# Top-32 attention and a gated MoE on one core: where the weight-decoding steps and the slot masks stand in the turns of the start-up

## The chip, the core and the metric

The kernel runs on one core of a Trainium2 chip, as a single program with one launch. The metric is the device time of that program in microseconds (us). The engines are TensorE (PE, with its weight loads as PEld), VectorE (DVE), ScalarE (ACT), GpSimd (POOL) and SyncE (SP, which here only issues DMAs). Each engine executes its own instructions strictly in the order in which the program lists them; between engines only semaphores order the work.

## The reference

Eight batches of eight heads, 576 positions, head size 64. Every query keeps its 32 best scores, and the attended values go through a product of two projections and two more projections:

```python
scores = q @ k.T / 8                      # per batch and head: 576 x 576
kth    = 32nd largest of each row
attn   = softmax(where(scores >= kth, scores, -1e9))
x      = (attn @ v)                       # gathered to 4608 x 512
h      = (x @ w1) * (x @ w2)              # 4608 x 1024
out    = (h @ w3) @ w_out                 # 4608 x 512
```

All inputs and the result are 32-bit floats.

## The kernel before

**Attention slots.** The work of the attention is cut into 144 slots of 128 queries for two streams of scores (a pair of heads, or the two ends of a pair of pairs). The main loop (line 529) makes one turn for each `p` from -1 to 146, and a turn works on four slots at once, at four different stages. In this document turn n is the pass with p = n. For slot p (`top32_steps`, lines 245 to 272), DVE reduces the scores to three sorted sets and takes eight maxima four times. For slot p - 1, POOL makes the two bounds of a row, `edge` (line 274), ACT and POOL make the mask (`mask`, line 301: a Relu on ACT, then a subtraction on POOL, once for each half), ACT takes the exponentials with their sums (`exps`, line 306), POOL adds 1e-9 to the sums (`enlarge`), DVE inverts them (`invert`), and POOL multiplies (`normalise`, line 316). For slot p - 2, PE turns the weights (`turn`, tiles `tp` and `ro`), ACT copies them, PE forms the values, and ACT and DVE split these into a high and a low part, `xf`. For slot p + 1, PE forms the scores (`st`) and ACT copies them to `s`.

**Filling.** The MoE of a finished part of a batch (`moe_steps`, line 368, tiles `ab` and `eo`) is a generator of matmuls. `fill` (line 493) is called three times in a turn and lets as many matmuls of it onto PE as the table `SHARE` allows. The MoE can begin only when the weights are decoded.

**Weight units.** The weights arrive as 64-bit floats in 40 tiles `z` of 512 KB, fetched by SP three ahead (`prefetch`, line 509), into four buffers. Each tile is a *unit*: a generator that does one step whenever it is advanced. Its steps (`decode`, line 113, and the loaders at lines 142, 156 and 166) are, in order: for some units (`by_pool`) a scaling on POOL, `y<-z`, from which only the sign is used; two conversions on ACT, `t<-z` and `z<-z`; one or two bit operations on DVE, `y<-t` and `y<-t,y`; an addition on POOL, `y<-y,z` (or `wo<-y,z`); and for w1 and w2 a rounding on ACT, `wh<-y`, and a subtraction on POOL, `wl<-y,wh`. The w3 units are then multiplied with w_out on PE, in eight products `pf` for each of eight results, which ACT and DVE split into `wf`.

**Where the steps stand.** `warm` (line 514) starts at most one new unit and advances every unit under way by one step. It is called at five places of each turn (lines 547, 559, 566, 583 and 594), and in turn -1 at two of them (lines 583 and 594). Nothing else sets the order: what a call of `warm` emits goes to each engine ahead of all that the loop emits after it. The five places are: in the first stage, ahead of the masks of slot p - 1; behind `turn`; behind the second `fill`; behind `enlarge`, ahead of `normalise`; and at the end of the turn, behind `normalise`, so ahead of the `edge` of the next turn.

The start-up ends when the last unit has done its last step, between the `normalise` of turn 14 and the bounds of turn 15; from there on `warm` does nothing.

Of the kernel before, what the change touches and what calls it, by code (L numbers as in the profile page):

```python
# [60 lines left out]
def attn_moe(ctx: ExitStack, tc: tile.TileContext, q, k, v, w1, w2, w3, w_out, out, flag, general):  # L61
# [45 lines left out]
    def fetch(src):  # L107

        z = z_p.tile([128, 1024], F32, tag="z", name="z")
        sp.dma_start(z.bitcast(I32), src)  # L110
        return z
# [49 lines left out]
    def weigh(n):  # L161
        while heavy and n:
            heavy.pop(0)()
            n -= 1
# [31 lines left out]
    def load_qk(b, part, hp):  # L196

        lo, n, _ = PARTS[part]
        qt = kq_p.tile([128, NA], F32, tag="q", name="qt")
        sp.dma_start(qt[:, :n], at(q, b, hp)[:, lo : lo + n])  # L200
        kt = kq_p.tile([128, S + 64], F32, tag="k", name="kt")
        sp.dma_start(kt, at(k, b, hp))
        return qt, kt

    def load_v(b, hp):

        vt = kq_p.tile([128, 11 * D], F32, tag="v", name="vt")
        sp.dma_start(vt, at(v, b, hp))
        return vt
# [22 lines left out]
    def new_s():  # L232
        return att_p.tile([128, 2, S], F32, tag="s", name="s", bufs=2)

    def take_scores(s, st, h):
        lo, hi = KEYS[h]
        return act.copy(s[:, :, lo:hi], st[h][:, :, : hi - lo])
# [7 lines left out]
    def top32_steps(s, st, taken, slot):  # L245

        w = att_p.tile([128, 2, S], F32, tag="w", name="w", bufs=1)
        top = tops[slot % len(tops)]
        one, two, three = slice(0, NG), slice(NG, 2 * NG), slice(2 * NG, S)
        in_two, in_three = st[0][:, :, NG : 2 * NG], st[1][:, :, :NG]
        dve.tensor_tensor(w[:, :, three], s[:, :, one], in_two, op=ALU.max)
        dve.tensor_tensor(w[:, :, two], s[:, :, one], in_two, op=ALU.min)
        yield
        ins = dve.tensor_tensor(w[:, :, one], w[:, :, three], in_three, op=ALU.max)
        behind(ins, taken, "one engine at a time reads a bank of the scores")  # L260
        dve.tensor_tensor(w[:, :, three], w[:, :, three], in_three, op=ALU.min)
        yield
        for i in range(4):
            cut = slice(i * 8, (i + 1) * 8)
            for a in range(2):
                dve.max(top[:, a, cut], w[:, a, one] if i < 3 else w[:, a, :])
                if i == 3 and a == 0:
                    yield
            if i < 3:
                for a in range(2):  # L270
                    dve.match_replace(w[:, a, one], top[:, a, cut], w[:, a, one], NEG)
                yield

    def edges_of(slot):
        top = tops[slot % len(tops)]
        edge = small.tile([128, 2, 2], F32, tag="edge", name="edge")
        pool.tensor_tensor(edge, top[:, :, 0:32:31], coef, op=ALU.mult)
        return edge

    def compare(slot):  # L280
        top = tops[slot % len(tops)]
        pool.tensor_tensor(over[:, 2 * slot : 2 * slot + 2], top[:, :, 31], top[:, :, 23], op=ALU.subtract)
# [15 lines left out]
    def new_weights():  # L298
        return att_p.tile([128, 2, S], F32, tag="pab", name="pab"), small.tile([128, 2], F32, tag="sums", name="sums")

    def mask(s, edge, pab, a):

        act.activation(pab[:, a, :], s[:, a, :], AF.Relu, bias=edge[:, a, 1:2], scale=-STEEP)
        pool.tensor_tensor(pab[:, a, :], s[:, a, :], pab[:, a, :], op=ALU.subtract)

    def exps(edge, pab, sums, a):
        p = pab[:, a, :]
        act.activation(p, p, AF.Exp, bias=edge[:, a, 0:1], scale=SCALE, accum_out=sums[:, a : a + 1])
# [11 lines left out]
    def turn(pab):  # L320

        tp = ps_a.tile([128, 2, 512], F32, tag="a", name="tp")
        flat = pab[:].rearrange("p a c -> p (a c)")
        for a in range(2):
            for c in range(4):
                o = a * (S + 64) + c * 128
                pe.transpose(tp[:, a, c * 128 : (c + 1) * 128], flat[:, o : o + 128], ident)
        ro = ps_v.tile([128, 512], F32, tag="v", name="ro")
        pe.transpose(ro[:, :128], flat[:, 512:640], ident)
        return tp, ro  # L330

    def take_turned(tp, ro):
        pts = att_p.tile([128, 2, 512], F32, tag="pts", name="pts", bufs=1)
        act.copy(pts, tp)
        pr = att_p.tile([128, 128], F32, tag="pr", name="pr")
        act.copy(pr, ro[:, :128])
        return pts, pr
# [26 lines left out]
    def take_low(to, ov):  # L364
        for x, cols, n in to:
            dve.tensor_tensor(x[:, 1, cols], ov[:, n], x[:, 0, cols].bitcast(F32), op=ALU.subtract)
# [122 lines left out]
    def evict():  # L489
        while put_off:  # L490
            put_off.pop(0)()

    def fill(n):
        nonlocal spare
        evict()
        spare = spare + n if queue else 0
        while queue and spare > 0:
            cost = next(queue[0], None)
            if cost is None:
                queue.pop(0)  # L500
            elif not cost:
                spare = 0
            else:
                spare -= cost

    waiting = list(startup)
    fetched, going, turns = [], [], []

    def prefetch(n):
        while waiting and len(fetched) < n:  # L510
            src, step = waiting.pop(0)
            fetched.append((fetch(src), step))

    def warm(first=True):

        if p < 0 and not first:
            return
        turns.append(p)
        n = len(turns)
        if fetched and (n % 5 if n < 11 else n % 2) and len(going) < 5:  # L520
            z, step = fetched.pop(0)
            going.append(step(z))
        going[:] = [unit for unit in going if next(unit, "end") != "end"]
        prefetch(3)

    qk[units[0]] = load_qk(*units[0])
# [2 lines left out]
    for p in range(-1, n_slots + 3):  # L529
        i, j, m = p + 1, p - 1, p - 2  # L530
        if i < n_slots:
            for u in units:
                if first[u] - 2 == i:
                    qk[u] = load_qk(*u)
                if first[u] == i:
                    vts[u] = load_v(u[0], u[2])
        finder = top32_steps(ss[p], *sts.pop(p), p) if 0 <= p < n_slots else iter(())
        if 0 <= j < n_slots:
            edges[j] = edges_of(j)
        next(finder, None)  # L540
        if m - 1 in lows:
            take_low(*lows.pop(m - 1))
            b, part, _ = slots[m - 1][0][0]
            if final[b, part] == m - 1:
                queue.append(moe_steps(b, part, [xts.pop((b, part, hp)) for hp in range(NHP)], put_off.append))
        next(finder, None)
        if p >= 0:
            warm()
        if 0 <= j < n_slots:
            pabs[j] = new_weights()  # L550
            for a in range(2):
                mask(ss[j], edges[j], pabs[j][0], a)
            compare(j)
        fill(SHARE[0])
        next(finder, None)
        if 0 <= m < n_slots:
            tp, ro = turn(pabs[m][0])
            pts, pr = take_turned(tp, ro)
        warm(False)
        if 0 <= j < n_slots:  # L560
            exps(edges[j], *pabs[j], 0)
            exps(edges[j], *pabs[j], 1)
        weigh(1)
        fill(SHARE[1])
        next(finder, None)
        warm(False)
        if i < n_slots:
            st = scores([qk[u] for u in slots[i][0]], slots[i][1])
            ss[i] = new_s()
            take_scores(ss[i], st, 0)  # L570
            sts[i] = st, take_scores(ss[i], st, 1)
        if 0 <= m < n_slots:
            us, t = slots[m]
            for u in us:
                if u not in xts:
                    xts[u] = new_x()
            ov = values([vts[u] for u in us], t, pts, pr, ro)
            lows[m] = places([xts[u] for u in us], t), ov
            take_high(*lows[m])
        if 0 <= j < n_slots:  # L580
            enlarge(pabs[j][1])
        next(finder, None)
        warm()
        next(finder, None)
        if 0 <= j < n_slots:
            invert(pabs[j][1])
            normalise(*pabs[j])
        weigh(8)
        fill(SHARE[2])
        for _ in finder:  # L590
            pass
        if 0 <= m < n_slots:
            del ss[m], pabs[m], edges[m]
        warm()
# [62 lines left out]
```

## Time and profile before

| | |
|---|---|
| time, median of 3 runs | 1267.78 us (1266.63 to 1267.80) |
| the profiled execution's own time | 1266.87 us |
| its span, first to last instruction | 1264.9 us |
| PE busy | 1209.7 us (96%) |
| DVE busy | 1135.0 us (90%) |
| ACT busy | 943.4 us (75%) |
| POOL busy | 872.4 us (69%) |

The span is what the trace covers; the execution's own time is 2.0 us longer. Busy shares are means over the whole span, and the start-up of some 200 us looks different from the rest: the page's slices show PE at 3 to 8 tenths in the first six slices (of 31.6 us each), and at 9 in nearly all the later ones. An idle time in a listing stands in brackets behind the instruction that it precedes, with the operation that ended it.

### The profile page before, as it was taken

The numbers are of one execution on the slowest core, as the hardware profiler recorded it, in microseconds if no ns is written. First come the engines' busy times: TensorE is split into PE (matmuls) and PEld (weight loads), VectorE is DVE, ScalarE is ACT, GpSimd is POOL, SyncE is SP. The second block draws the span as 40 slices with busy tenths as digits, with TensorE's granted clock in tenths as the row PEclk, the third lists the DMA queues.
The fourth block names the chain that finished last, engine by engine and source line by source line (L and its number), as shares of the span: only waits on it lengthen the run. The fifth ranks groups of instructions, "written<-read, shape, count | busy, mean of one in ns | idle before, by whom it ended". The sixth has DMA issues, their size and how long they took to land.

```text
span 1264.9 us, 29916 instructions
## 1 busy us (share of the span) xinstructions
PE 1209.7 (96%) x10513; PEld 1043.5 (82%) x10513; DVE 1135.0 (90%) x3968; ACT 943.4 (75%) x2025; POOL 872.4 (69%) x1213
## 2 busy tenths in 40 slices
PE   3788889999999999999999999999999999999998
PEld 1444568888888888888888888888888888888898
DVE  7897979999999999999999999999999999999910
ACT  5887877777777777777777777777777777777731
POOL 5887887676766767676766767676766767676731
PEclk9999989999999999999999999999999999999999
DMA  7533421202112121202112121202112111202000
GB/s 236 174 129 130 156 70 40 91 27 70 55 39 90 36 63 40 90 28 70 55 39 91 36 63 40 90 28 70 55 39 91 35 63 40 91 27 70 13 22 21
DMA packets 42803, 85.92 MB, mean 68 GB/s; under 512 B 4754, under 2 KB 21138, under 8 KB 42642
## 3 DMA queue, kind: packets, MB, share of 16 engines
q1 hardware_dynamic: 42642, 83.91, 20.6%
q8 instruction: 85, 1.39, 0.5%
q14 instruction: 76, 0.62, 0.2%
HBM read 74.45 MB, written 9.44 MB: 66 GB/s over the span
## 4 chain that ended last, share of the span: by engine, by line
PE 75%; POOL 10%; DVE 7%; ACT 4%; issue 3%; DMA 1%; SPq 0%; DVEq 0%; POOLq 0%; ACTq 0%
PE ab L52 27%; PE eo L52 15%; PE ro L52 12%; PE st L52 11%; PE tp L52 9%; POOL pab L52 5%; DVE w L52 3%; DVE top L52 2%; ACT pab L52 2%; PE pf L52 2%; POOL y L52 2%; POOL g L52 1%; DVE y L52 1%; POOL wl L52 1%; ACT pts L52 1%
## 5 line engine op out<-in xcount | busy, mean ns | idle before, releaser
L52 POOL TENSOR_TENSOR pab<-s,pab 128x576 f32<-128x576 f32 x288 | 404.8, 1427 | 121.9 <-ACT pab L52 121.9
L52 DVE MAX8 top<-w 128x8 f32<-128x192 f32 (+1 forms) x1152 | 478.5, 448 | 0.0
L52 PE MATMUL ab<-xf,wh 128*128 128x256 f32 (+1 forms) x2048 | 438.5, 302 | 10.1 <-DVE y L52 8.7
L52 PEld LDWEIGHTS ab<-xf,wh 128*128 128x128 f32 x2048 | 332.9, 189 | 21.6 <-DVE y L52 9.5
L52 ACT ACTIVATE pab<-s,edge 128x576 f32<-128x576 f32 x288 | 208.0, 769 | 176.6 <-POOL edge L52 176.6
L52 PE MATMUL ab<-xf,wl 128*128 128x256 f32 (+1 forms) x1024 | 307.4, 300 | 0.0
L52 DVE MATCH_REPLACE8 w<-top,w 128x192 f32<-128x192 f32 x864 | 289.7, 343 | 0.0
L52 POOL TENSOR_SCALAR pab<-pab,sums 128x576 f32<-128x576 f32 x288 | 212.6, 751 | 78.0 <-DVE sums L52 78.0
L52 ACT ACTIVATE pab<-pab,edge 128x576 f32<-128x576 f32 x288 | 223.1, 779 | 11.9 <-POOL pab L52 9.7
L52 PE MATMUL eo<-g,wf 128*128 128x256 f32 (+1 forms) x1536 | 231.6, 301 | 0.0
L52 PEld LDWEIGHTS eo<-g,wf 128*128 128x128 f32 x1536 | 208.5, 188 | 8.1 <-issue 7.5
L52 PEld LDWEIGHTS ab<-xf,wl 128*128 128x128 f32 x1024 | 193.4, 189 | 4.1 <-issue 4.1
L52 PE MATMUL st<-kt,qt 64*128 64x192 f32 (+3 forms) x1280 | 182.8, 435 | 9.8 <-DMA kt<-in_k 4.8
L52 ACT COPY pts<-tp 128x1024 f32<-128x1024 f32 x144 | 145.6, 1011 | 46.8 <-PE tp L52 44.3
L52 ACT COPY s<-st 128x768 f32<-128x768 f32 (+1 forms) x288 | 169.9, 646 | 5.8 <-PE st L52 5.8
L52 PE MATMUL tp<-ident,pab 128*128 128x128 f32 x1152 | 153.8, 278 | 14.2 <-DVE w L52 9.5
L52 PEld LDWEIGHTS st<-kt,qt 64*128 64x128 f32 (+1 forms) x1280 | 97.9, 178 | 83.7 <-issue 18.6
L52 DVE TENSOR_TENSOR w<-w,st 128x384 f32<-128x384 f32 x288 | 158.2, 549 | 4.9
L52 PE MATMUL ro<-pts,vt 128*64 128x128 f32 (+1 forms) x2560 | 161.2, 269 | 1.0 <-ACT pr L52 1.0
L52 DVE TENSOR_TENSOR w<-s,st 128x384 f32<-128x384 f32 x288 | 146.7, 551 | 14.0
L52 POOL TENSOR_TENSOR g<-whole,g 128x256 fp32r<-128x256 f32 (+1 forms) x128 | 103.3, 807 | 78.6 <-ACT g L52 78.6
L52 PEld LDWEIGHTS ro<-pts,vt 128*64 128x64 f32 x2560 | 127.5, 137 | 34.4 <-issue 24.2
(47 smaller groups left out, 1128.7 us busy)
## 6 DMA issues: line engine op xcount, KB each, us to landing
vt<-in_v SPq DMA_DIRECT2D x64, 352.0 KB, 3.2
kt<-in_k SPq DMA_DIRECT2D x64, 320.0 KB, 3.8
z<-in_w SPq DMA_DIRECT2D x32, 512.0 KB, 3.8
qt<-in_q SPq DMA_DIRECT2D x32, 160.0 KB, 3.2
out_t<-osb SPq DMA_DIRECT2D x32, 160.0 KB, 1.8
z<-in_wo SPq DMA_DIRECT2D x8, 512.0 KB, 5.2
qt<-in_q SPq DMA_DIRECT2D x32, 128.0 KB, 3.1
out_t<-osb SPq DMA_DIRECT2D x32, 128.0 KB, 1.7
```

The source lines that it names most:

```text
L52: ins = fn(*args, **kw)
```

## The change

Three things are changed, all in the order of emission; no instruction is added or taken away.

- In `warm`, a newly started unit does its first step ahead of the steps of the older units, where before it came last.
- In the first stage of a turn, the masks of slot p - 1 and the small `compare` on POOL come ahead of the call of `warm`, where before they came behind it.
- In turn -1 only the call at the end of the turn remains, so that one unit has been started ahead of slot 0 where before there were two. All later starts thereby move by one call of `warm`.

```diff
@@ warm
         turns.append(p)
-        n = len(turns)
+        n, new = len(turns), None
         if fetched and (n % 5 if n < 11 else n % 2) and len(going) < 5:
             z, step = fetched.pop(0)
-            going.append(step(z))
+            new = step(z)
+            next(new)
         going[:] = [unit for unit in going if next(unit, "end") != "end"]
+        if new:
+            going.append(new)
         prefetch(3)
@@ first stage of a turn
         next(finder, None)
-        if p >= 0:
-            warm()
         if 0 <= j < n_slots:
             pabs[j] = new_weights()
             for a in range(2):
                 mask(ss[j], edges[j], pabs[j][0], a)
             compare(j)
+        if p >= 0:
+            warm()
         fill(SHARE[0])
@@ last stage of a turn
             enlarge(pabs[j][1])
         next(finder, None)
-        warm()
+        if p >= 0:
+            warm()
         next(finder, None)
```

How this moves instructions is shown on POOL at three places. There `edge` are the bounds of a slot, `pab<-s,pab` its two masks, `sums<-sums` its `enlarge`, and `pab<-pab,sums` its `normalise`; rows with `z`, `wl` or `wo` are steps of units.

POOL in turn 3, from the bounds to the `enlarge`, before:

```order
L52 TENSOR_TENSOR edge_395<-top2_100,coef_93 128x4
L52 TENSOR_TENSOR pab_406<-s_270,pab_406 128x576 x2
L52 TENSOR_TENSOR over_96<-top2_100 128x2
L52 TENSOR_TENSOR wl00_106<-y_348,wh0_101 128x512
L52 TENSOR_TENSOR y_389<-y_389,z_282 128x512
L52 TENSOR_SCALAR y_434<-z_309 128x512
L52 TENSOR_SCALAR sums_407<-sums_407 128x2
```

and now:

```order
L52 TENSOR_TENSOR edge_388<-top2_100,coef_93 128x4
L52 TENSOR_TENSOR pab_396<-s_266,pab_396 128x576 x2
L52 TENSOR_TENSOR over_96<-top2_100 128x2
L52 TENSOR_TENSOR y_373<-y_373,z_254 128x512
L52 TENSOR_SCALAR y_439<-z_335 128x512
L52 TENSOR_TENSOR wl00_106<-y_373,wh0_101 128x512
L52 TENSOR_TENSOR y_403<-y_403,z_290 128x512
L52 TENSOR_SCALAR sums_397<-sums_397 128x2
```

The scaling of the new unit (`y_434<-z_309`, now `y_439<-z_335`) has moved ahead of the two steps of older units, and a further addition (`y_373`) that stood ahead of the bounds now stands behind the masks.

POOL from a `normalise` to the masks of the next turn, before, at the change from turn 6 to turn 7:

```order
L52 TENSOR_SCALAR pab_740<-pab_740,sums_741 128x576 x2
L52 TENSOR_TENSOR wl00_106<-y_734,wh0_101 128x512
L52 TENSOR_TENSOR y_777<-y_777,z_666 128x512
L52 TENSOR_SCALAR y_830<-z_707 128x512
L52 TENSOR_TENSOR edge_838<-top0_98,coef_93 128x4
```

and now, at the change from turn 5 to turn 6:

```order
L52 TENSOR_SCALAR pab_620<-pab_620,sums_621 128x576 x2
L52 TENSOR_SCALAR y_711<-z_596 128x512
L52 TENSOR_TENSOR wl00_106<-y_627,wh0_101 128x512
L52 TENSOR_TENSOR y_664<-y_664,z_543 128x512
L52 TENSOR_TENSOR edge_720<-top2_100,coef_93 128x4
```

The same three steps stand between the `normalise` and the bounds, one turn earlier, and the scaling is now the first of them. At the change from turn 6 to turn 7 none is left between the two.

POOL from the `normalise` of turn 13 to the `enlarge` of turn 14, before:

```order
L52 TENSOR_SCALAR pab_1535<-pab_1535,sums_1536 128x576 x2
L52 TENSOR_TENSOR g_1404<-whole_1641,g_1404 128x320
L52 TENSOR_TENSOR edge_1658<-top1_99,coef_93 128x4
L52 TENSOR_TENSOR wl11_1602<-y_1578,wh1_102 128x512
L52 TENSOR_TENSOR y_1633<-y_1633,z_1461 128x512
L52 TENSOR_TENSOR pab_1672<-s_1469,pab_1672 128x576 x2
L52 TENSOR_TENSOR over_96<-top1_99 128x2
L52 TENSOR_TENSOR wl11_1602<-y_1633,wh1_102 128x512
L52 TENSOR_TENSOR y_1668<-y_1668,z_1516 128x512
L52 TENSOR_SCALAR sums_1673<-sums_1673 128x2
```

and now:

```order
L52 TENSOR_SCALAR pab_1524<-pab_1524,sums_1525 128x576 x2
L52 TENSOR_TENSOR g_1396<-whole_1635,g_1396 128x320
L52 TENSOR_TENSOR wl11_1627<-y_1531,wh1_102 128x512
L52 TENSOR_TENSOR y_1596<-y_1596,z_1433 128x512
L52 TENSOR_TENSOR edge_1655<-top1_99,coef_93 128x4
L52 TENSOR_TENSOR pab_1663<-s_1461,pab_1663 128x576 x2
L52 TENSOR_TENSOR over_96<-top1_99 128x2
L52 TENSOR_TENSOR wl11_1627<-y_1596,wh1_102 128x512
L52 TENSOR_TENSOR y_1649<-y_1649,z_1487 128x512
L52 TENSOR_SCALAR sums_1664<-sums_1664 128x2
```

The two steps that stood between the bounds and the masks stand ahead of the bounds now; the number of steps from the `normalise` to the `enlarge` is the same.

Counted over the `normalise` of turns 1 to 14, 22 unit steps of POOL stood between one of them and the next masks; now it is 13.

On PE the order changes only in the `pf` products of the start-up: they come in groups of other sizes, the last eight all in turn 11, where four of the last eight stood in turn 10. The first `ab` matmul stands between the `tp` of turns 11 and 12 in both, and from there on PE's order is the same. From turn 16 on no engine's order differs.

## Rows read from the trace of the kernel before

**Rows 1.** Stretches: from:to, length, busy (instructions) of PE, PEld, DVE, ACT, POOL; clock, DMA.
```profile
47.00:124.00 77.00, 66.83 (x371) 34.82 (x368) 66.06 (x197) 59.12 (x118) 61.85 (x74) 0.96 0.43 142
124.00:171.00 47.00, 38.98 (x235) 27.34 (x233) 43.19 (x129) 39.26 (x78) 41.68 (x47) 0.93 0.44 140
...
201.00:1264.90 1063.90, 1056.31 (x9598) 946.90 (x9596) 962.51 (x3447) 792.99 (x1730) 712.97 (x1020) 1.00 0.17 53
```

**Rows 2.** Waits of DVE from 8 to 201 us: total us, times, longest.
```profile
DVE y L52 <- ACT t L52: 13.9, 5, 8.2
DVE sums L52 <- POOL sums L52: 4.0, 5, 2.2
DVE y L52 <- POOL y L52: 3.2, 2, 2.5
DVE y L52 <- ACT xf L52: 2.5, 1, 2.5
DVE wf L52 <- ACT wf L52: 1.3, 2, 0.8
DVE whole L52 <- ACT asb L52: 1.0, 1, 1.0
```

**Rows 3.** Timeline of DVE, rows with idle time before them: start, us, instruction, [idle <-releaser].
```profile
49.93 0.69 DVE L52 SCALAR_TENSOR_TENSOR y<-t,y 128x512 int32<-128x512 int32 x1 [2.47 <-POOL y L52]
...
88.02 0.69 DVE L52 TENSOR_TENSOR wf<-pf,wf 128x512 fp32r<-128x512 f32 x1 [0.77 <-ACT wf L52]
...
92.17 0.69 DVE L52 TENSOR_SCALAR y<-t 128x512 int32<-128x512 int32 x1 [0.51 <-ACT t L52]
...
108.08 0.69 DVE L52 TENSOR_SCALAR y<-t 128x512 int32<-128x512 int32 x1 [2.30 <-ACT t L52]
...
120.57 0.69 DVE L52 SCALAR_TENSOR_TENSOR y<-t,y 128x512 int32<-128x512 int32 x1 [2.46 <-ACT xf L52]
...
164.57 0.69 DVE L52 TENSOR_SCALAR y<-t 128x512 int32<-128x512 int32 x1 [1.90 <-ACT t L52]
...
169.90 0.69 DVE L52 TENSOR_SCALAR y<-t 128x512 int32<-128x512 int32 x1 [0.95 <-ACT t L52]
...
181.24 0.17 DVE L52 RECIPROCAL sums<-sums 128x2 f32<-128x2 f32 x1 [2.23 <-POOL sums L52]
...
191.42 0.17 DVE L52 RECIPROCAL sums<-sums 128x2 f32<-128x2 f32 x1 [0.88 <-POOL sums L52]
```

**Rows 4.** Timelines of ACT and DVE at the start: the first copy of scores, the first comparison.
```profile
6.50 1.18 ACT L52 COPY s<-st 128x768 f32<-128x768 f32 x2 [4.49 <-PE st L52]
...
9.57 1.01 DVE L52 TENSOR_TENSOR w<-s,st 128x384 f32<-128x384 f32 x2
```

**Rows 5.** Timeline of POOL in turn 3.
```profile
46.71 1.28 POOL L52 TENSOR_TENSOR wl<-y,wh 128x512 fp32r<-128x512 f32 x1
47.94 1.30 POOL L52 TENSOR_TENSOR y<-y,z 128x512 int32<-128x512 int32 x1
49.21 0.69 POOL L52 TENSOR_SCALAR y<-z 128x512 f32<-128x512 f32 x1
```

**Rows 6.** Timeline of POOL: the bounds and the masks of turn 7.
```profile
88.85 0.21 POOL L52 TENSOR_TENSOR edge<-top,coef 128x4 f32<-128x4 f32 x1
89.94 2.79 POOL L52 TENSOR_TENSOR pab<-s,pab 128x576 f32<-128x576 f32 x2 [0.89 <-ACT pab L52]
```

**Rows 7.** Waits of POOL from 8 to 201 us.
```profile
POOL pab L52 <- ACT pab L52: 8.1, 10, 1.3
```

**Rows 8.** Timeline of PE: seven products (two records each); the first `ab`.
```profile
129.42 6.28 PE L52 MATMUL pf<-wo,y 128*128 128x512 f32 x14
...
145.71 0.56 PE L52 MATMUL ab<-xf,wh 128*128 128x320 f32 x2 [2.99 <-DVE y L52]
```

**Rows 9.** Timeline of PE: the eight turning matmuls of turns 3 and 4.
```profile
41.50 1.94 PE L52 MATMUL tp<-ident,pab 128*128 128x128 f32 x8 [5.56 <-DVE w L52]
...
54.40 1.06 PE L52 MATMUL tp<-ident,pab 128*128 128x128 f32 x8
```

## Prediction

> **What bounds the kernel now.** I read the busy times by stretch first [rows 1]. From 201 us on PE is busy 1056.31 of 1063.90 us, and its order there is not touched: this part costs what it did. From 47 to 171 us PE, DVE, ACT and POOL are all busy 77% to 92% of their time: PE 66.83 of 77.00 us in the first stretch, DVE 66.06, then DVE 43.19 of 47.00. No engine is full, so waits between them set the time. So the change can only move the moment at which the start-up hands over to the PE-bound part.
>
> The waits of DVE come second [rows 2]. Without the 8.2 us before its first instruction, DVE waits 5.7 + 4.0 + 3.2 + 2.5 + 1.3 + 1.0 = 17.7 us up to 201 us: for the conversions of units (`t`), for the sums, for POOL's scalings, and for `wf`. None of these is a wait at the first instruction of a turn, for scores: DVE paces the turns, and what delays it is what the turns last too long. 17.7 us, and what the start can give, is the ceiling of a gain. The timeline [rows 3] gives nearly all of the 17.7 us one by one, each with its cause.
>
> POOL comes third, because DVE's waits mostly end at it: 61.85 of 77.00 us [rows 1] in a ring that DVE closes (`edge`, masks, `enlarge`, the inversion on DVE, `normalise`, the next `edge`).
>
> **The change part by part.** No instruction is added or removed, so the sum has only waits in it.
>
> *Start.* The first comparison of scores begins at 9.57 us, though the copy that it needs ends at 6.50 + 1.18 = 7.68 [rows 4]: two operations of the first unit, 0.69 us each [rows 3], come first. Now they follow. DVE begins 1.9 us earlier and does 1.4 us of unit work later: **-0.5 us**. Ends: 0 (the unit is late again later) and -1.9.
>
> *Scalings.* The wait of 2.47 us at 49.93 ends with POOL's scaling at 49.21, which stood behind a `wl` of 1.28 and an addition of 1.30 us [rows 5]. Now the new unit comes first, so 2.55 us earlier. The wait of 2.46 us at 120.57 is put down to ACT, but has the same form (the second DVE operation of a scaled unit), and I count it here. Of the 3.2 us that DVE waits for POOL's `y` [rows 2] another 0.7 is left, a third such scaling. In all 5.6 us: I take **-5.0**, since the third one now stands behind masks. Ends: -5.6, and 0 if the next wait of the ring merely moves up.
>
> *Masks first.* At 108.08 DVE waits 2.30 us for a conversion that stands behind exponentials, which were held back by masks behind unit steps. Three more waits for sums are short: 4.0 us in all less the 2.23 and 0.88 of the two long ones leave 0.9 [rows 2, 3]. There, too, unit steps stood ahead of the masks or of `enlarge`. I take **-2.9** of these 3.2 us; ends -3.2 and 0.
>
> *The shift by one call.* Here is what the change costs. Steps in the last call of a turn stand between `normalise` and the next `edge`, and the masks wait for them. From turn 6 to turn 7 three steps (1.28 + 1.30 + 0.69 us by [rows 5]) put the bounds off to 88.85 us [rows 6], and DVE then waits 0.77 and 0.51 us [rows 3]; from turn 12 to turn 13 two steps do, and it waits 1.90 and 0.95. So such a place costs 1.28 to 2.85 us, 2.1 in the mean, and there were two. The new order has three with two or more steps (from turn 5 to 6, 11 to 12 and 13 to 14, the start aside): one more, **+2.1**. Ends: -4.1 if earlier bounds elsewhere absorb them all, +4.4 if the three cost 2.85 each.
>
> *Sums.* The steps that stood ahead of the masks now stand behind them, so ahead of `enlarge`, where DVE's inversion waits. Turn 14 shows it: the same number of steps from `normalise` to `enlarge`, so the 2.23 us at 181.24 are not removed. Elsewhere one or two steps of 1.3 us come between. The nearest price is the short wait for sums in sight, 0.88 us at 191.42 [rows 3]; I take three such turns, **+2.6**. Ends: 0, and three times 2.23 = +6.7.
>
> *What moves at no cost.* On ACT, masks now wait for `edge` where conversions filled the time before, but ACT has most slack (59.12 of 77.00 us) [rows 1]. SP issues the same DMAs, one call later, three units ahead: units are taken up later, not sooner, so no fetch is asked for earlier; if that cover went, a fetch of the start would be waited for, inside the 8 to 47 us where DVE shows none. PE has four more `pf` products ahead of its first `ab` in turn 11, of 6.28 / 7 = 0.9 us each; it waits 2.99 us for DVE there now [rows 8], which covers all but 0.6 of their 3.6 us, and without that cover the 3.6 us would put off the turning of turn 12. The last unit ends one call later, behind the first `ab`, which needs only the first halves.
>
> Sum: -0.5 - 5.0 - 2.9 + 2.1 + 2.6 = -3.7 us. The profiled execution took 1266.87 us, so it would take 1263.2; the median of the runs is 0.9 us higher, and I forecast **1264.0 us** for it.
>
> *A rule weighed.* PE's eight turning matmuls take 1.94 us behind a wait of 5.56 us and 1.06 us where it had been busy [rows 9]; the granted clock is 0.96 and 0.93 in the mean of the two stretches, so some spells ran at 1.2 in place of 2.4 GHz [rows 1], and PE lost 0.04 x 77 + 0.07 x 47 = 6.4 us of full-speed work there. These lie beside DVE's work, and I count none. The Trainium skill ("TensorE: Matmul & The Clock Gate", Part 1) says that the array's clock is gated down by default, and that activity releases it. By that rule fewer waits would give clock back too, and the rows agree that slow matmuls stand behind waits; whether it shortens a turn, no row here shows.
>
> **The rivals.**
>
> *A larger gain.* Both removals hold in full, the places of the shift cost nothing, and no sums come late: -0.5 - 5.6 - 3.2 - 4.1 = -13.4, so 1254.4 us. For it speaks that 13 steps stand between `normalise` and masks where 22 stood. Against it: POOL has 15.15 us idle in the 77 [rows 1], and its ring leaves little of it free.
>
> *PE's clock comes back as well.* If the turns were paced by PE's slow matmuls, the 6.4 us would come on top: -10.1, so 1257.7 us. Against it: DVE's waits name ACT and POOL, never PE.
>
> *The waits only move.* What DVE no longer waits for at a scaling it waits for at the inversion, because POOL's ring is as long as a turn: the removals (-7.9) are paid back by three inversions at 2.23 us and the extra place, +6.7 + 2.1: within 1 us of 1267.8. For it: after the 2.47 us at 49.93 the next thing DVE needs are those very sums.
>
> *Slower: POOL stands idle ahead of every mask.* With masks first, POOL has nothing to do while ACT makes the first half of the Relu, 0.89 us [rows 6]. Today it waits so 10 times, 8.1 us in all [rows 7], in 16 turns; in every turn it is 16 x 0.89 = 14.2, so 6.1 us more. If POOL's ring decides every turn, that is added, with the shift and the sums, and only start and scalings are gained: +6.1 + 2.1 + 2.6 - 0.5 - 5.0 = +5.3, so 1273.1 us. It decides once POOL has less than 0.4 us a turn (6.1 over 16) left; it has 15.15 us in some 6.5 turns now [rows 1], so most of that would have to go to other waits.
>
> *The change does nothing.* The units may be late by other things: 1267.8 us.
>
> **How the numbers follow.** Forecast (a gain of 2.5 to 7.5 us): 0.42. Larger gain: 0.12. With the clock: 0.04. Waits only move: 0.26. Nothing: 0.02. Slower: 0.14. A measurement of this kernel can tell about 0.2% from no change, 2.5 us. Faster by more than that: 0.42 + 0.12 + 0.04 = 0.58; within it: 0.26 + 0.02 = 0.28; slower: 0.14. The range reaches from 1257, which holds the clock's case and about half of the larger gain, to 1270, which holds the moved waits whole and the milder part of the slower case: what is left out is some 0.06 below and 0.10 above, with a little for other things. The faster cases alone would span 1257 to 1265.
>
> **What would show it.** Right: no wait of over 1 us of DVE for a POOL scaling; the conversion behind the exponentials in turn 8 without its 2.30 us; DVE's waits from 8 to 201 us at 12 to 15 us in place of 17.7; the first turn without a wait of DVE for sums or units some 4 us earlier; the stretch behind it as long as now. The costs right: waits of 1 to 2.5 us in turns 6, 12 and 14, and inversions waiting for sums in three more turns. Wrong: waits for sums of over 10 us in all, or turns longer than now from 60 to 170 us; PE waiting for anything but DVE and POOL in turns 11 and 12; or a difference that arises behind the start-up, where I expect none.

## The result and the profile after

The changed kernel takes 1285.63 us in the median of 4 runs (1285.16 to 1288.09), the kernel before 1267.36 us beside it: a ratio of 1.0148 with an interval of 1.0134 to 1.0162, so some 18 us slower. The forecast was 1264.0 us and the range ended at 1270. The profiled execution was the longest of the four, 1288.09 us with a span of 1285.6 us, so what the two traces differ by (20.7 us in the span) is a little more than the medians do.

The busy times of the changed kernel by stretch, in the columns of [rows 1]:

```profile
47.00:124.00 77.00, 64.70 (x333) 34.45 (x332) 63.15 (x189) 54.89 (x109) 57.68 (x68) 0.88 0.39 128
124.00:171.00 47.00, 40.13 (x231) 23.14 (x228) 38.46 (x120) 33.74 (x68) 34.94 (x41) 0.89 0.42 134
171.00:220.00 49.00, 35.43 (x268) 30.31 (x269) 37.79 (x120) 35.00 (x73) 39.02 (x47) 0.90 0.26 83
220.00:1285.60 1065.60, 1057.61 (x9608) 948.41 (x9606) 963.56 (x3448) 792.07 (x1730) 712.25 (x1021) 1.00 0.17 53
```

Behind the start-up nothing changed: PE is busy 1057.61 of 1065.60 us, as it was 1056.31 of 1063.90 [rows 1]. The loss lies ahead of it. In the same 47 us from 124 on every engine but PE does less than before: DVE 38.46 us where it did 43.19, POOL 34.94 where it did 41.68. The granted clock of PE has fallen from 0.96 and 0.93 to 0.88 and 0.89.

The waits of DVE from 8 to 220 us (total us, times, longest), which answer to [rows 2]:

```profile
DVE y L52 <- ACT t L52: 12.1, 9, 3.2
DVE wf L52 <- ACT wf L52: 9.1, 5, 3.0
DVE w L52 <- ACT s L52: 6.2, 3, 2.8
DVE sums L52 <- POOL sums L52: 3.3, 3, 1.7
DVE xf L52 <- ACT xf L52: 2.4, 3, 1.1
DVE y L52 <- POOL y L52: 1.8, 1, 1.8
DVE sums L52 <- ACT xf L52: 1.1, 1, 1.1
DVE whole L52 <- ACT asb L52: 0.7, 1, 0.7
DVE y L52 <- POOL wo L52: 0.7, 1, 0.7
DVE y L52 <- POOL wl L52: 0.5, 1, 0.5
```

They come to 37.9 us, where there were 17.7 without the wait before DVE's first instruction: 20.2 us more, about what the span grew by (1285.6 - 1264.9 = 20.7). Two of the waits stand out: the one for `wf`, the split of PE's products of the weights, has grown (9.1 us, before 1.3 [rows 2]), and the one at the start of turns, for the scores `s`, is new (6.2 us, before none).

Followed back, both lead round a ring of POOL, ACT and PE. The waits of these three from 8 to 220 us:

```profile
POOL pab L52 <- ACT pab L52: 30.3, 16, 4.9
...
ACT wf L52 <- PE pf L52: 17.2, 5, 5.2
PE pf L52 <- POOL y L52: 16.2, 4, 7.0
...
ACT s L52 <- PE st L52: 9.4, 3, 4.5
```

POOL waits 30.3 us for the Relu of its masks (8.1 before, up to 201 us [rows 7]), in the mean 1.9 us each. In eight of the 16 turns it is the 0.89 us of a Relu alone [rows 6]; in the other eight, all from turn 4 to turn 12, it is 1.9 to 4.9 us. PE waits 16.2 us for additions of units, which it needs for its products; ACT waits 17.2 us for these products.

Turns 7 and 8 show such a ring. POOL first:

```profile
94.09 0.20 POOL L52 TENSOR_TENSOR edge<-top,coef 128x4 f32<-128x4 f32 x1
98.11 2.78 POOL L52 TENSOR_TENSOR pab<-s,pab 128x576 f32<-128x576 f32 x2 [3.82 <-ACT pab L52]
100.85 0.20 POOL L52 TENSOR_TENSOR over<-top 128x2 f32<-128x2 f32 x1
101.02 0.66 POOL L52 TENSOR_SCALAR y<-z 128x512 f32<-128x512 f32 x1
101.63 1.28 POOL L52 TENSOR_TENSOR wl<-y,wh 128x512 fp32r<-128x512 f32 x1
102.85 1.30 POOL L52 TENSOR_TENSOR y<-y,z 128x512 int32<-128x512 int32 x1
...
112.73 1.42 POOL L52 TENSOR_TENSOR pab<-s,pab 128x576 f32<-128x576 f32 x1 [4.06 <-ACT pab L52]
```

ACT in the same time:

```profile
96.26 0.59 ACT L52 CAST wf<-pf 128x512 fp32r<-128x512 f32 x1 [2.90 <-PE pf L52]
96.74 0.62 ACT L52 CAST wh<-y 128x512 fp32r<-128x512 f32 x1
97.26 1.44 ACT L52 ACTIVATE pab<-s,edge 128x576 f32<-128x576 f32 x2
...
107.97 1.18 ACT L52 COPY s<-st 128x768 f32<-128x768 f32 x2 [4.46 <-PE st L52]
...
111.90 1.43 ACT L52 ACTIVATE pab<-s,edge 128x576 f32<-128x576 f32 x2
```

And PE:

```profile
104.21 2.07 PE L52 MATMUL pf<-wo,y 128*128 128x512 f32 x2 [7.00 <-POOL y L52]
106.21 2.29 PE L52 MATMUL st<-kt,qt 64*128 64x384 f32 x8
```

POOL has its bounds at 94.3 us and then stands idle 3.82 us, since ACT's Relu is queued behind a `wf` that waits for PE. Before, the same three unit steps (the scaling, the `wl` and the addition) stood at the end of turn 6, ahead of these bounds, and POOL waited 0.89 us for the masks [rows 6]. The third part moves them one call later, between the bounds and the masks, and the second part puts them behind the masks, so that nothing fills the wait. So the addition ends at 104.15, and PE, which has idled 7.00 us, begins the product that reads it at 104.21. The scores of the next slot stand behind that product on PE, at 106.21; ACT waits 4.46 us for them; the next Relu comes after the copy, at 111.90; and the next masks wait 4.06 us. Here what POOL loses ahead of a mask comes back to it one turn later as the next late Relu. It does not go on for ever: ahead of the masks of turn 9 POOL waits 0.89 us again.

At the start, DVE's first comparison comes earlier, as expected (9.57 before [rows 4]):

```profile
6.90 1.02 DVE L52 TENSOR_TENSOR w<-s,st 128x384 f32<-128x384 f32 x2 [6.90 <-ACT s L52]
```

By turn 2 that lead is gone: its first comparison is at 31.87 us, where it was at 30.57.

### The profile page after: what moved, and what is told of

It reads as the page before. It is cut to its first block, busy times and chain, and to the rows that moved or that the text cites. A ratio compares the mean times of both kernels' runs of the same rounds, so it can differ in the third digit from the quotient of the medians.

```text
span 1285.6 us, 29919 instructions
## 1 busy us (share of the span) xinstructions
PE 1216.2 (95%) x10513; PEld 1046.4 (81%) x10513; DVE 1136.3 (88%) x3968; ACT 942.2 (73%) x2025; POOL 870.3 (68%) x1213
## 4 chain that ended last, share of the span: by engine, by line
PE 81%; POOL 6%; DVE 5%; ACT 5%; issue 2%; DMA 1%; SPq 0%; DVEq 0%; ACTq 0%; POOLq 0%
PE ab L52 29%; PE eo L52 15%; PE ro L52 13%; PE st L52 12%; PE tp L52 9%; PE pf L52 3%; POOL pab L52 3%; DVE w L52 2%; ACT pab L52 2%; DVE top L52 2%; POOL y L52 1%; DVE y L52 1%; ACT pts L52 1%; POOL g L52 1%; POOL wl L52 1%
## 5 line engine op out<-in xcount | busy, mean ns | idle before, releaser
L52 PEld LDWEIGHTS ab<-xf,wh 128*128 128x128 f32 x2048 | 332.6, 188 | 25.4 <-ACT asb L52 10.5
L52 PE MATMUL st<-kt,qt 64*128 64x192 f32 (+3 forms) x1280 | 186.7, 441 | 22.8 <-DVE w L52 9.8
L52 PE MATMUL tp<-ident,pab 128*128 128x128 f32 x1152 | 151.0, 274 | 8.6 <-DVE w L52 7.4
```

The source lines that it names most:

```text
L52: ins = fn(*args, **kw)
```

## The experiments

Runs of one group shared the runs of the kernel before. A time difference is taken against the median of these; the interval is that of the ratio.

### The parts alone

The first three kernels each have one part of the change's diff: the edit in `warm`; the edit in the first stage; the edit in the last stage. The fourth has the first two.

```
e1: new = step(z); next(new)   # ahead of the older units' steps
e2: mask(...), compare(j)      # ahead of warm()
e3: if p >= 0: warm()          # the call behind enlarge
e4: e1 and e2
```

> Only the first part of the change: a new unit's first step ahead of the older units' steps; calls and masks as before. Late operands (the loss comes from unit additions that now stand behind the masks, for which PE's products wait in their order): this part leaves the additions where they were, 1264 to 1269 us. Shifted calls (the loss comes from the one call fewer in turn -1, which moves every later step by one call): no shift here, 1264 to 1269 us. My prediction's accounting (only DVE's waits count): 5 us of waits for scalings gone, 1261 to 1264 us.

> Only the second part: the masks of a slot ahead of the first call of warm in a turn. Late operands: most of the loss, 1274 to 1284 us, with PE waiting over 10 us for POOL additions ahead of the products. Shifted calls: 1264 to 1270 us. My prediction's accounting: 1263 to 1266 us.

> Only the third part: one call of warm in turn -1 in place of two. Late operands: only what is lost at the start, 1269 to 1273 us. Shifted calls: most of the loss, 1277 to 1287 us. My prediction's accounting: the extra place ahead of the bounds and the later sums, 1270 to 1273 us.

> The first two parts without the third: new step first and masks first, but two calls in turn -1 as before. Late operands: 1274 to 1284 us. Shifted calls: 1262 to 1270 us, so nearly all of the 18 us gone. My prediction's accounting: 1259 to 1262 us.

Measured, against 1267.22 us: e1 1265.49 us (ratio 0.9985, 0.9976 to 0.9995), e2 1282.98 (1.0122, 1.0105 to 1.0138), e3 1273.52 (1.0050, 1.0033 to 1.0067), e4 1282.46 (1.0115, 1.0097 to 1.0132). So -1.7, +15.8 and +6.3 us, in sum +20.3 against +18.3 for the whole. The masks carry most of the loss, and the first part is a small gain.

### Which queue: ACT's or POOL's

In e5 only ACT's order changes: the two Relus come ahead of the units' steps, POOL's subtractions stay behind them.

```diff
+        if 0 <= j < n_slots:
+            pabs[j] = new_weights()
+            for a in range(2):
+                act.activation(pabs[j][0][:, a, :], ss[j][:, a, :], AF.Relu, bias=edges[j][:, a, 1:2], scale=-STEEP)
         if p >= 0:
             warm()
...
-                mask(ss[j], edges[j], pabs[j][0], a)
+                pab = pabs[j][0][:, a, :]
+                pool.tensor_tensor(pab, ss[j][:, a, :], pab, op=ALU.subtract)
```

> The mask is split: ACT's two Relus ahead of the first call of warm, POOL's two subtractions and the compare behind it, as before. Idle gap (with masks first POOL has nothing to do between the bounds and the end of the first Relu, and ACT nothing before the bounds): the unit steps of POOL fill the gap again, 1262 to 1269 us. Late operands (additions behind POOL's masks are late for PE's products): the additions stand ahead again, 1262 to 1269 us. Order on ACT (unit steps behind Relus that wait for the bounds): nothing is repaired, 1276 to 1284 us.

In e6 only POOL's order changes: each unit names the engine of its next step, and in the first call of a turn POOL's steps are kept back until the masks are emitted.

```diff
         if p >= 0:
-            warm()
+            warm(late=True)
...
             compare(j)
+        if p >= 0:
+            advance(rest)
+            rest.clear()
+            prefetch(3)
```

> The counterpart: in the first call of a turn the unit steps of ACT and DVE stay ahead of the masks, those of POOL alone come behind them; ACT's and PE's orders are as before. Idle gap: POOL's part of it is there again, 1274 to 1282 us. Late operands: all of the loss, 1277 to 1284 us. Order on ACT: 1264 to 1270 us.

Measured, against 1266.99 us: e5 1267.31 (1.0000, 0.9991 to 1.0010), e6 1284.92 (1.0141, 1.0124 to 1.0158), so +17.9 us. The waits of e6 from 8 to 215 us:

```profile
POOL pab L52 <- ACT pab L52: 30.9, 16, 6.4
PE pf L52 <- POOL y L52: 28.1, 6, 11.8
```

And those of e5:

```profile
ACT pab L52 <- POOL edge L52: 25.8, 14, 3.1
...
POOL pab L52 <- ACT pab L52: 8.8, 12, 0.9
```

In e5 ACT waits 25.8 us for the bounds and nothing is lost by it. The whole cost of the second part comes from POOL's order: in the trace of e6 the instructions of ACT, DVE and PE stand in the order of before, and those of POOL in the order of e2. That e6 is 2.1 us above e2 lies within the two intervals.

### Late additions or idle ahead of the masks

In e7 PE's products read the decoded w_out tile in place of the unit's result, so that PE waits for no addition; e8 is the same with the masks first.

```diff
-                fold[f], y[:, (j % 4) * 128 : (j % 4 + 1) * 128], wo[:, j * DM : (j + 1) * DM],
+                fold[f], wo[:, (j % 4) * 128 : (j % 4 + 1) * 128], wo[:, j * DM : (j + 1) * DM],
```

> The kernel before, with the products of w3 and w_out reading a decoded tile of w_out in place of the unit's own tile: PE's products wait for no unit addition, the count of matmuls is the same, and the folded weight is not w3 times w_out. This is the reference for the next kernel. All theories: 1262 to 1268 us, since DVE and not PE paces most turns of the kernel before.

> The second part of the change (masks first) with the same free products, so again not w3 times w_out; to be set against the kernel before with free products. Late operands: PE's waits for POOL are gone, and the masks cost 0 to 5 us. Idle gap: 11 to 16 us as ever. Order on ACT: 11 to 16 us as ever.

Measured: e7 1266.91 us (0.9999, 0.9990 to 1.0009), e8 1276.12 (1.0069, 1.0052 to 1.0085). With free products the masks cost 9.2 us (e8 less e7), with the real ones 15.8. So about 6.6 us of them go through the additions that PE waits for; the intervals of e2 and e8 leave 2.5 to 11 us. The waits of POOL for its masks in e8:

```profile
POOL pab L52 <- ACT pab L52: 20.3, 17, 3.9
```

In e7 they are 10.5 us. The 9.8 us more agree with the 9.2 us of time, which is an agreement of two sizes and no proof; no run took this idle away alone with the masks still first. How it reaches the turns, the waits of DVE in e8 show:

```profile
DVE sums L52 <- POOL sums L52: 8.2, 6, 2.8
DVE y L52 <- POOL y L52: 7.5, 3, 4.3
```

In e7 these are 4.2 and 3.2 us. The unit steps behind the masks make POOL's `enlarge` late, and a scaling behind the masks is late itself: 8.3 us of the 8.9 by which DVE's waits grow from e7 to e8. With the real products (e2) the same two have grown as much or more, from 4.0 and 3.2 us:

```profile
DVE y L52 <- POOL y L52: 9.7, 4, 4.3
DVE sums L52 <- POOL sums L52: 8.5, 5, 3.5
```

### What the missing call costs

The third part leaves out a unit ahead of slot 0, and it shifts the places of all later starts. e9 has the first without the second, e10 the second without the first; e11 has one call more in place of one fewer, and e12 this together with the first part of the change.

```
e9:  if p >= 0: warm() else: turns.append(p)     # the call behind enlarge
e10: n = len(turns) - 1, with a start at n == 0 too
e11: warm() also in the first stage of turn -1
e12: e11 and e1
```

> Only the third part, changed so that the places of the starts within the turns stay those of the kernel before: the call at the end of turn -1 starts and advances nothing but is counted, so one unit is under way ahead of slot 0 instead of two, and every later unit takes the place that the unit before it had. Theory 'the missing unit': the third part's 6.3 us come from having one unit less ahead of slot 0 (everything one start later), so this too takes 1272 to 1277 us. Rival 'the places': they come from where the steps fall within a turn (between the normalise and the bounds, behind the masks); then this is within 3 us of the kernel before, 1264 to 1270 us.

> Both calls of turn -1 as before, so two units are under way ahead of slot 0, but from turn 0 on the starts stand at the places that the third part gives them (every later unit one call later than the places of before and one start earlier than in the third part). Theory 'the missing unit': within 3 us of the kernel before, 1264 to 1270 us. Rival 'the places': 4 to 8 us above it, 1271 to 1275 us.

> The opposite of the third part: one call more in turn -1, so the later starts move by one call the other way. Theory 'the missing unit': an earlier unit helps or costs nothing, 1260 to 1268 us. Rival 'the places': another set of places, with the three steps of turns 5 to 6 and 11 to 12 moved again, so a change of either sign of up to 6 us; over 1270 us speaks for it.

> A version that may beat the kernel before: the first part of the change (a new unit's first step ahead of the others) with one call more in turn -1. If the two gains add, 1.7 us of the first part on top of whatever one call more gives: 1258 to 1266 us. If one call more only changes the places for the worse, 1268 us or more.

Measured, against 1267.16 us: e9 1271.28 (1.0032, 1.0020 to 1.0044), e10 1271.85 (1.0046, 1.0033 to 1.0060), e11 1274.00 (1.0055, 1.0041 to 1.0069), e12 1270.45 (1.0024, 1.0015 to 1.0033). e9 lies between what the two theories said, and e10 and e11 speak for the places. Both halves of the third part cost something, 4.1 and 4.7 us, together less than their sum. The first comparisons of turns 10 and 17 in e9 show how the missing unit comes back:

```profile
119.44 1.02 DVE L52 TENSOR_TENSOR w<-s,st 128x384 f32<-128x384 f32 x2
...
204.84 1.02 DVE L52 TENSOR_TENSOR w<-s,st 128x384 f32<-128x384 f32 x2
```

Before, they begin at 123.89 and 200.47 us: e9 is 4.5 us ahead at turn 10 and 4.4 us behind at turn 17. That fits a unit that is not done ahead of slot 0 and is done in the last turns of the start-up instead.

Do the places cost because unit steps put off the bounds, as the prediction had it? e13, e14 and e15 (the kernel before, the third part, the first part) emit the bounds ahead of the last call of a turn:

```diff
-        if 0 <= j < n_slots:
-            edges[j] = edges_of(j)
         next(finder, None)
...
             del ss[m], pabs[m], edges[m]
+        if 0 <= p < n_slots:
+            edges[p] = edges_of(p)
```

> The kernel before with the bounds of a slot emitted ahead of the last call of a turn, so ahead of the unit steps that stand between a normalise and the bounds; the masks stay behind those steps. Theory 'late bounds cost': the two places with several steps (turns 6 to 7 and 12 to 13) get cheaper, 1.3 to 2.9 us each, so 1261 to 1265 us. Rival 'only the masks matter': POOL has the same work between normalise and masks, so 1266 to 1269 us; it could be slower where POOL now waits for the maxima of DVE ahead of its unit steps.

> The third part (one call fewer ahead of slot 0) with the same move of the bounds. Theory 'late bounds cost': most of the 6.3 us of the third part goes away, 1265 to 1269 us. Rival 'only the masks matter': 1272 to 1276 us, as the third part alone.

> The first part of the change (new units' first steps ahead of the others) with the move of the bounds: a version that may beat the kernel before. If the 1.7 us of the first part and a gain of e13 add: 1260 to 1264 us; if the bounds give nothing, 1264 to 1267 us.

Measured, against 1266.46 us: e13 1267.08 (1.0004, 0.9995 to 1.0013), e14 1274.09 (1.0049, 1.0036 to 1.0063), e15 1266.29 (0.9995, 0.9986 to 1.0004). Earlier bounds change nothing, with the third part or without it, so late bounds by themselves are not what costs. It is also what the rival 'only the masks matter' expected: in these kernels the masks still stand behind the same unit steps on POOL, and what that costs was not taken apart.

The trace of e3 offered two more. Its waits from 8 to 215 us:

```profile
PE ab L52 <- ACT asb L52: 11.5, 2, 7.0
...
PE pf L52 <- POOL y L52: 8.0, 3, 4.7
```

In e16 the third part gets an earlier eviction of `ab`; in e17 it gets the free products of e7; e18 is the first part of the change with the earlier eviction.

```diff
         warm(False)
+        if p < 16:
+            evict()
         if 0 <= j < n_slots:
             exps(edges[j], *pabs[j], 0)
```

> The third part with one more edit: in the turns up to 15 the pending eviction of the MoE (the copy of `ab` on ACT, in turns 11 and 12, and what goes with it in turn 13) is emitted ahead of the slot's exponentials, which themselves wait for late masks, and no longer behind them. In the trace of the third part the exponentials ahead of the longest such wait take 1.6 us and wait for nothing; so theory 'ab waits for its eviction, and the next scores behind it' expects 2 to 5 us less than the third part alone: 1268 to 1271 us. Rival 'the additions of the units': no change, 1272 to 1275 us.

> The third part with products that read the decoded w_out tile in place of the unit's own result, so that they wait for no addition of a unit; the products then do not compute w3 x w_out, and the output is not the reference's. Theory 'the additions of the units': PE's 8.0 us of waits for them go, and the time falls by 3 to 5 us to 1268 to 1270 us. Rival 'ab waits for its eviction': 1272 to 1275 us, as the third part alone.

> The first part of the change (new units' first steps ahead of the others) with the early eviction in the turns up to 15. PE waits 1.4 us for the eviction in the kernel before, so at most 1 to 2 us on top of the first part's 1.7: 1263 to 1266 us; 1266 us or more if the copy on ACT now holds back the exponentials.

Measured, against 1267.26 us: e16 1273.83 (1.0043, 1.0029 to 1.0057), e17 1273.99 (1.0055, 1.0041 to 1.0069), e18 1265.68 (0.9984, 0.9975 to 0.9993). Without PE's wait for additions the third part costs what it did: that theory falls, for this part. The eviction is inconclusive. It took the wait down only a little, as e16's row shows, and the time by less than the intervals can tell:

```profile
PE ab L52 <- ACT asb L52: 10.0, 2, 5.5
```

What the places cost by stays open. All five orders that move the starts (e3, e9 to e12) are slower, by 3.3 to 6.8 us, and neither the bounds nor the products explain it. Their traces do show where it arises: the first comparison of turn 10 begins at most 1.4 us later than before in any of the five, that of turn 17 4.0 to 6.8 us later. Between the two the MoE starts, and in all five PE then waits longer for its eviction, 3.4 to 7.0 us at a time, where it waited 1.4 before. In e3:

```profile
160.89 0.90 PE L52 MATMUL ab<-xf,wh 128*128 128x320 f32 x2 [4.50 <-ACT asb L52]
...
183.75 0.90 PE L52 MATMUL ab<-xf,wh 128*128 128x320 f32 x2 [7.00 <-ACT asb L52]
```

This makes the late eviction a likely part of the cost, but it is not shown: e16 hardly shortened the wait.

No version tried beats the first part alone by more than the runs can tell: e1 at 1265.49 us and e18 at 1265.68 are both about 0.15% faster than the kernel before.

## Why the prediction was wrong

**The step that failed** is the second part: *Masks first* at -2.9 us with *Sums* at +2.6, and above all *What moves at no cost*. The prediction looked at ACT, which would wait for the bounds, and called that free. This was right (e5: 25.8 us of such waits, no loss). It did not follow the steps that are moved behind the masks on POOL. It counted them against the next inversion on DVE alone. With the masks alone (e2) DVE's waits for `sums` did grow, by 4.5 us, so this term was right in kind and too small; the waits for conversions, from which *Masks first* hoped to gain, grew as well, from 13.9 to 18.0 us. But the results of the steps are awaited elsewhere too. DVE itself waits for the scalings, 6.5 us more in e2. An addition `y<-y,z` of a w3 unit is awaited by PE's next product, and behind that in PE's order stand the scores of the next slot, for which ACT and DVE wait. In the whole change the first part takes the wait for scalings away again (1.8 us), the waits for `sums` are 3.3 us, and it is the way through PE that grows. The price of the second part was put at -2.9 + 2.6 = -0.3 us; the masks alone measured +15.8, and POOL's order alone +17.9.

**The rival with the right sign** was *Slower: POOL stands idle ahead of every mask*, at a chance of 0.14. Its place was right: 16 waits in 16 turns, as it said. Its price was not. It took the Relu at 0.89 us a turn, 6.1 us in all, where POOL's waits grew by 9.8 us with free products (e8 against e7) and to 30.3 us in the changed kernel. A Relu that waits in ACT's queue for PE, which waits for POOL, is not 0.89 us away. Its chance was set low because POOL has 15.15 us idle in 77 [rows 1]. That was no slack: in the changed kernel POOL is idle 77 - 57.68 = 19.3 us in the same stretch, and it still holds up the turns, for the idle time lies where nothing behind it may pass.

*Scalings* (-5.0): the first part alone gave -1.7 us, between nothing and the forecast. In its trace DVE waits no more for POOL's `y` (3.2 us before) nor for the `xf` that was counted with it (2.5), but for sums 6.1 us in place of 4.0 and for `t` 16.3 in place of 13.9, up to 215 us. So the waits were read rightly, 5.7 us of them went, and 4.5 came back elsewhere. Here the rival *The waits only move* was the better account.

*Start* (-0.5): right in kind. DVE's first comparison comes 2.7 us earlier, where 1.9 was said; it is the third part that does it (e3: 7.02 us, e1: 9.49).

*The shift by one call* (+2.1, with -0.5 of the start in the same edit): the third part measured +6.3 us, so the sign was right and the size low. The mechanism named had two halves, late bounds and the masks behind them; the bounds by themselves cost nothing (e13, e14), and the masks' share is open. The price was also misread in part: the wait of 0.77 us that ends at 88.02 us [rows 3] was put down to bounds that POOL only makes at 88.85 [rows 6]. That the last unit may end later at no cost is in doubt as well: in e9, where the units take the places of before but each one start later, the time grew by 4.1 us, though this moves every unit and not the last alone.

*Four more products ahead of the first `ab`*: the first `ab` no longer waits for DVE [rows 8]. What PE waits for later is the eviction of `ab`, in turn 12 already, one of the signs that the prediction had named for being wrong:

```profile
162.12 0.85 PE L52 MATMUL ab<-xf,wh 128*128 128x320 f32 x2
...
172.90 0.56 PE L52 MATMUL ab<-xf,wh 128*128 128x320 f32 x2 [2.84 <-ACT asb L52]
...
197.20 0.90 PE L52 MATMUL ab<-xf,wh 128*128 128x320 f32 x2 [7.12 <-ACT asb L52]
```

*Behind the start-up*: right. Two turns later the distance between the kernels no longer changes (turn 17 begins 20.05 us later than before, turn 18 20.06).

*The clock*: the granted clock fell from 0.96 to 0.88 in the stretch from 47 to 124 us, so PE spent more of it at 1.2 in place of 2.4 GHz. The product at 104.21, behind 7.00 us without work, took 2.07 us, where seven in a row took 0.90 each [rows 8]; the granted clock from 104.0 to 106.3 us was 0.50, the lower of the two. Here the scores stood right behind it, so at least 1.2 us of slow matmul lay on the path. The prediction's sum counted none of this, and its rival on the clock had it as a gain alone. How much of the 18 us is the clock's no run shows. The Trainium skill ("TensorE: Matmul & The Clock Gate", Part 1) says that the array's clock is gated down by default and that activity releases it; the trace agrees, with 0.88 where PE waits more.

## What to carry to other kernels

A filler step in an in-order queue has two costs to look up before it is moved: what stands behind it on its own engine, and who waits for its result, followed through every engine on which that waiter has something queued. Filler steps ahead of an instruction that must wait for another engine are not a delay but a use of that wait; behind it, they become late by the whole wait. Idle time of an engine in a ring is no slack unless the instructions that could use it stand ahead of the wait, and a wait's price is taken with the queue in front of its releaser, not from the releaser's own duration.

## What was not expected

Nothing of the hardware itself beyond the clock's part above. In the order, the size was not expected: 14 of POOL's 1213 instructions at another place in its queue, with none added and no other engine's order changed, cost 17.9 us (e6).
